# k and q of two head pairs handled together, six first-layer blocks held in SBUF, and a second phase that begins with results in SBUF, in a planned attention and feed-forward kernel

## The chip, the cores and the metric

The kernel runs on one core of a Trainium2 chip. The metric is device time in microseconds (us) of one execution. The engines are TensorE (PE in the profile; its weight loads are PEld), VectorE (DVE), ScalarE (ACT), GpSimd (POOL) and SyncE (SP), on whose queue all DMAs are issued. SBUF is the memory on the chip, PSUM holds what matmuls accumulate, and DRAM is outside.

## The reference

A linear attention over 8 batches, 8 heads, 576 positions and 64 columns per head, and then a feed-forward layer on its 4608 tokens of 512 columns, all in float32:

```python
q_s = softmax(q, axis=-1)            # over the 64 columns
k_s = softmax(k, axis=2)             # over the 576 positions of a batch
kv = einsum('bhsd,bhse->bhde', k_s, v)
x = einsum('bhsd,bhde->bhse', q_s, kv)     # then heads side by side: (4608, 512)
h = x @ w_in                               # 512 x 2048
g = where(h >= 1, h, where(h <= -1, 0, (h + 1) ** 2 / 4))
out = g @ w_out                            # 2048 x 512
```

## The kernel before

**Tiles.** The 4608 tokens are nine chunks of T = 512. A chunk's x is four pieces, one for each pair of heads (128 columns). The first layer makes h transposed, in 16 blocks f of 128 of the 2048 columns; the second layer adds each block into four PSUM banks o0 to o3 of 128 tokens by 512 columns. To keep float32 accuracy every operand is split into a rounded high part and the low rest, and a product is three matmuls (high x low, high x high, low x high). So one block's second layer is 4 banks x 3 matmuls of 128x512 (L1439), and its first layer in a plain chunk 4 pieces x 3 (L1240). In a row of the trace gh and gl are the parts of g, wh and wl those of w_out, qh and ql those of q.

**Stages.** Chunks 0, 1 and 2 are done plainly. In chunk 0 `weights` loads w_in and w_out from the inputs, splits them and stores the w_in blocks (512 KB each) to DRAM copies; chunks 1 and 2 fetch these again. While they do, `split` makes sums of weight blocks, ss, and their parts w_s (casts on ScalarE, L591; low parts on GpSimd, L596), which go to DRAM too. Chunks 3 to 8 are three pairs: `two_first_layers` makes the first layers of both chunks of a pair with seven instead of eight products (Strassen's scheme; tiles hA, hb, hC), out of sums of x. For these the chunks' x (xo, stored to xk by L963) is loaded again into xc by `x_sums` (L1143), combined (L1158), cast to its high part on ScalarE (L1170) and given its low part (L1175). The x parts lie in fourteen places x0 to x13 of SBUF, which chunks 0 to 2 also use: chunk 2's four pieces lie in x10 to x13, so that the first pair's x10 to x13 can be written only when chunk 2's last first layer has read them. Of a pair only the first chunk's g goes straight into the second layer. The second chunk's is spilled to DRAM (`keep`, L1400), loaded again (`recall`, L1411) and multiplied in a second phase, 16 blocks of 12 matmuls, behind the pair's products. It uses the same four banks, which `evict` copies into osb tiles first (two buffers; L379 on ScalarE, L381 on VectorE) and stores (L1497): the third copy needs the first one's store to have landed.

**Attention of a piece** (`attention`, from chunk 2 on). k's maximum over a batch's rows is taken in two steps: k_max over five column groups in three operations of VectorE (L724, L726, L727), and then over the partitions, for chunks 2 to 4 through two transposes on TensorE with a reduction between (L765, L769, L773), for chunks 5 and on by a `partition_all_reduce` on GpSimd (L776). Then k_sub (L780, VectorE), k's exponential (L785, ScalarE), the kv matmuls (L795, ten for each head pair; two pairs share one PSUM tile), 1/sum (L810, L812) and the two parts of kv (L829, L840). q's maximum and sum go over 32 partitions' groups: a reduction (L873, L891), four copies of 32 partitions and one combination (q_both, L861 and L862), the application on GpSimd (L882), exponential (L887), reciprocal (L899, L904), a transpose (L908), its two parts (L923, L927), the x matmuls (L939), and x's parts (L952 on ScalarE, L956 on VectorE).

**The order.** All instructions are written out by a planner (`Plan`). Each operation has an engine, a duration in us, a due time and what it depends on; buffers are `Ring`s. `order` makes a list schedule, and `settle` shifts the order for 450 turns (`late`, `early`), moving some operations near one point of time at random each turn, within the first 120 us of the plan. Transfers are planned with 2.6 us ahead of the first byte and 310 KB per us. Engines work in this order; a late instruction holds those queued behind it.

## Time and profile before

| what | value |
|---|---|
| runs shown | 868.74, 870.13 and 870.80 us, median 870.13 |
| the profiled execution, its own time | 870.23 us |
| its span in the trace | 868.5 us |
| TensorE busy | 842.0 us, 97% of the span |
| VectorE, ScalarE, GpSimd busy | 554.7, 478.4 and 298.3 us |
| mean granted TensorE clock | 0.991 |
| DMA | 172.70 MB |

In the views a row of waits gives the engine, its line, whom it waited for, the total, the number of times and the longest. A row of the timeline gives start and duration, engine, line, operation, output and inputs by the program's names (without the number of the buffer), and in brackets the idle time before it with what ended it. A row of a stretch gives the busy time (and count) of PE, PEld, DVE, ACT and POOL, then the granted clock, the DMA engines' busy share and GB/s.

### The profile page before, as it was taken

How to read it: one execution, taken by the hardware profiler on the slowest of the kernel's cores; microseconds unless marked ns; L12 is line 12 of the kernel's file. 1: busy time of each engine (PE TensorE's matmuls, PEld its weight loads, DVE VectorE, ACT ScalarE, POOL GpSimd, SP SyncE). 2: the span in 40 equal slices, each digit the busy share in tenths (PEclk: the TensorE clock that was granted, in tenths of full speed). 3: DMA queues.
4: the chain of work that ended last, by engine and by line, in shares of the span. 5: the costliest groups of instructions: out<-in, count | busy, mean ns of one | idle time of the engine just before them, and what ended most of it. 6: DMA issues, size and time to landing. Idle time of an engine off the chain costs nothing.

```text
span 868.5 us, 12535 instructions
## 1 busy us (share of the span) xinstructions
PE 842.0 (97%) x4272; PEld 685.4 (79%) x4272; DVE 554.7 (64%) x1199; ACT 478.4 (55%) x842; POOL 298.3 (34%) x265
## 2 busy tenths in 40 slices
PE   8999998999999997999999899999999999999998
PEld 6678777888887776788878788888887888888886
DVE  7788788888787745887699454777763024554300
ACT  7888745555545536565568344556574344545522
POOL 5656544344537314211212321112256730000153
PEclk9999999999999998999999999999999999999999
DMA  8999936646576527666757634557456335454332
GB/s 329 293 310 331 318 137 231 219 170 200 203 255 217 184 98 247 238 204 237 237 172 227 234 121 165 182 171 240 171 185 228 122 122 169 161 168 146 112 118 86
DMA packets 68176, 172.70 MB, mean 199 GB/s; under 512 B 7568, under 2 KB 7824, under 8 KB 68112
## 3 DMA queue, kind: packets, MB, share of 16 engines
q1 hardware_dynamic: 68112, 171.90, 58.0%
q8 instruction: 34, 0.56, 0.3%
q14 instruction: 30, 0.25, 0.1%
HBM read 126.78 MB, written 45.09 MB: 198 GB/s over the span
## 4 chain that ended last, share of the span: by engine, by line
PE 80%; DVE 8%; DMA 7%; ACT 2%; POOL 2%; issue 2%; POOLq 0%; SPq 0%; DVEq 0%; ACTq 0%
PE o L1439 38%; PE hA L1292 14%; PE h L1240 10%; PE hC L1292 7%; PE hb L1292 3%; PE x L939 3%; DMA st<-in_w 2%; PE kv L795 2%; DMA out<-osb 1%; DMA k<-in_k 1%; DMA xk<-xo 1%; PE warm L1612 1%; DVE qrzo L861 1%; DVE gl L1428 1%; DVE m L726 1%
## 5 line engine op out<-in xcount | busy, mean ns | idle before, releaser
L1439 PE MATMUL o<-wl,gh 128*128 128x512 f32 x576 | 229.0, 398 | 8.6 <-ACT gh L1423 4.7
L1439 PE MATMUL o<-wh,gl 128*128 128x512 f32 x576 | 226.6, 393 | 1.4 <-DVE gl L1428 1.2
L1439 PE MATMUL o<-wh,gh 128*128 128x512 f32 x576 | 225.5, 391 | 0.0
L1240 PE MATMUL h<-x,w 128*128 128x512 f32 x576 | 147.5, 399 | 4.1 <-DVE x L956 2.4
L1292 PE MATMUL hA<-x,w 128*128 128x512 f32 x576 | 147.3, 392 | 1.2 <-DVE c L1316 1.2
L1439 PEld LDWEIGHTS o<-wl,gh 128*128 128x128 f32 x576 | 109.0, 189 | 33.2 <-ACT gh L1423 5.4
L1439 PEld LDWEIGHTS o<-wh,gl 128*128 128x128 f32 x576 | 108.8, 189 | 27.8 <-DVE gl L1428 3.9
L1240 PEld LDWEIGHTS h<-x,w 128*128 128x128 f32 x576 | 107.0, 190 | 28.4 <-DVE x L956 3.0
L1292 PEld LDWEIGHTS hA<-x,w 128*128 128x128 f32 x576 | 107.3, 188 | 24.8 <-DVE c L1316 2.0
L1439 PEld LDWEIGHTS o<-wh,gh 128*128 128x128 f32 x576 | 109.0, 189 | 21.6
L1428 POOL TENSOR_TENSOR gl<-gs,gh 128x512 fp32r<-128x512 f32 x39 | 50.3, 1291 | 165.7 <-PE o L1439 122.6
L1384 ACT ACTIVATE r<-r 128x512 f32<-128x512 f32 x144 | 90.9, 632 | 3.9
L882 POOL TENSOR_TENSOR q<-q,qrz 128x512 f32<-128x512 f32 x36 | 39.6, 1101 | 107.3 <-DVE qrz L904 65.6
L1292 PE MATMUL hC<-x,w 128*128 128x512 f32 x288 | 73.8, 391 | 0.4 <-DVE gl L1428 0.3
L882 POOL TENSOR_TENSOR q<-q,qm 128x512 f32<-128x512 f32 x36 | 39.5, 1100 | 91.2 <-DVE qm L862 39.0
L1423 ACT CAST gh<-gs 128x512 fp32r<-128x512 f32 x48 | 29.9, 622 | 72.9 <-PE o L1439 57.5
L1381 ACT ACTIVATE r<-c,half 128x512 f32<-128x512 f32 x48 | 34.7, 722 | 60.8 <-DVE c L1316 60.7
L1292 PEld LDWEIGHTS hC<-x,w 128*128 128x128 f32 x288 | 53.7, 188 | 13.1 <-DVE gl L1428 1.7
L1381 ACT ACTIVATE r<-h,half 128x512 f32<-128x512 f32 x48 | 33.0, 687 | 48.9 <-PE h L1240 48.7
L1316 DVE TENSOR_TENSOR c<-hC,sn_P 128x512 f32<-128x512 f32 x24 | 16.6, 690 | 56.3 <-PE hC L1292 56.3
L1175 POOL TENSOR_TENSOR x<-xc,x 128x512 fp32r<-128x512 f32 x27 | 35.5, 1327 | 33.6 <-ACT x L1170 26.1
L1387 DVE SCALAR_TENSOR_TENSOR h<-h,r 128x512 f32<-128x512 f32 x48 | 33.1, 691 | 20.1 <-ACT r L1384 19.9
(126 smaller groups left out, 1241.2 us busy)
## 6 DMA issues: line engine op xcount, KB each, us to landing
w<-b SPq DMA_DIRECT2D x56, 512.0 KB, 4.6
w<-s SPq DMA_DIRECT2D x48, 512.0 KB, 3.6
st<-in_w SPq DMA_DIRECT2D x32, 512.0 KB, 6.1
g<-c SPq DMA_DIRECT2D x48, 256.0 KB, 2.6
gs<-g SPq DMA_DIRECT2D x48, 256.0 KB, 2.6
v<-in_v SPq DMA_DIRECT2D x32, 325.0 KB, 5.4
q<-in_q SPq DMA_DIRECT2D x36, 256.0 KB, 3.4
out<-osb SPq DMA_DIRECT2D x35, 256.0 KB, 3.3
```

The source lines that it names most:

```text
L795: nc.tensor.matmul(t["kv"][d, :], t["k"][r, j, d], t["v"][r, j, i * (D + 1) : (i + 1) * (D + 1)], start=(j == 0), stop=(j == KJ - 1), tile ...
L882: nc.gpsimd.tensor_tensor(t["qf"], t["qf"], at, alu)
L939: nc.tensor.matmul(t["x"][:, :, p0:p1], lhs, rhs[:, :, p0:p1], start=(i == 0), stop=(i == 2),)
L1175: eng.tensor_tensor(x[:, 1, :], t["xc"][:, at, :], f32(x[:, 0, :]), ALU.subtract)
L1240: nc.tensor.matmul(t["h"], lhs, rhs, start=(at == 0 and i == 0), stop=(at == NPAIR - 1 and i == 2),)
L1292: nc.tensor.matmul(banks[b]["h"], lhs, rhs, start=(begins and not kk and not m), stop=(ends and kk == 1 and m == 2), skip_group_check=True,)
L1381: nc.scalar.activation(t["r"], t["h"], AF.Relu, bias=half[:, :1], scale=0.5)
L1384: nc.scalar.activation(t["r"], t["r"], AF.Square)
L1387: nc.vector.scalar_tensor_tensor(t["h"], t["h"], 1.0, t["r"], ALU.max, ALU.min)
L1423: nc.scalar.copy(t["gh"], t["h"])
L1428: eng.tensor_tensor(t["gl"], t["h"], f32(t["gh"]), ALU.subtract)
L1439: nc.tensor.matmul(outs[c, j], lhs[:, s], rhs, start=(f == 0 and i == 0), stop=(f == NF - 1 and i == 2),)
```

## The change

1. **Two head pairs as one piece.** From chunk 2 on `attention_two` takes the place of `attention`. k_max is one tensor_reduce for each head pair. The second reduction (k_top), the sum and reciprocal of kv, q_both's copies (now on 32 columns) and q's reciprocal are done once for two pairs. A piece's two all-reduces stand one behind the other on GpSimd. Loads and due times are arranged anew (k 45 us ahead of q in the pairs; chunk 2's pieces are entered within chunk 1).
2. **HELD.** Blocks 1, 3, 5, 7, 9 and 11 of w_in are written in chunk 0 to the x places x10, x11, x12, x13, x8 and x9 and used in chunk 1 from there; their six loads of 512 KB go.
3. **The second phase** begins with blocks 14 and 15, whose g stays in SBUF: two stores and two loads of 256 KB less in each of the three pairs. Then follow blocks 0 to 13.
4. **The planner** adds a margin of 1.2 us to the end of stores to DRAM copies and of loads from them; a few durations are set anew; `settle` picks its point near a planned idle time of TensorE, by its length, anywhere in the plan.

The issued DMAs go from 473 to 455; the matmuls are the same.

```diff
+HELD = {1: 10, 3: 11, 5: 12, 7: 13, 9: 8, 11: 9}
...
-    TURNS, SEARCHED = 450, 120.0
+    TURNS = 450
 
     PATIENCE = 0.2
 
-    RELUCTANT = 3.0
+    RELUCTANT, MARGIN = 3.0, 1.2
...
+        op.margin = self.MARGIN
+        return op
...
+                op.end = self.gap([used["wire"]], us, op.start + self.FIRST) + us + op.margin
...
-                about = rng.uniform(0.0, self.SEARCHED)
+                pe = sorted((o.start, o.end) for o in order if o.engine == "PE")
+                idle = [(b[0], b[0] - a[1]) for a, b in zip(pe, pe[1:]) if b[0] > a[1] + 0.05]
+                about = rng.choices([x for x, _ in idle], [x for _, x in idle])[0]
+                about -= rng.uniform(0.0, 8.0)
...
+                if f in HELD:
+                    flat = x_room(HELD[f]).rearrange("p i t -> p (i t)")
+                    wr[0, f] = wr[1, f] = flat.rearrange("p (q i t) -> p q i t", q=2, i=2)
+                else:
+                    ws_tile((0, f))
...
+        late = START + STEP * (NF - 2 + f) if f in HELD else due
+        made["stored", f] = plan.save(0.45, late, store, [g], 512)
...
+            if c == 1 and f in HELD:
+                made[c, f] = made[f, 0]
+            else:
+                made[c, f] = fetch((c, f), due - 1.5 * STEP, blocks[f], [made["stored", f]])
...
+    def attention_two(c, h, kdue, qdue):
+
+        two = 2 * h, 2 * h + 1
+        n = f"{c}_{h}"
+        t = {pr: {} for pr in two}
+        b = {}
...
+        def k_max(i):
+            def emit():
+                if not i:
+                    b["m"] = wk.tile([P, 2, P], F32, tag="m2", name=f"m2_{n}")
+                k = t[two[i]]["k"].rearrange("p j d -> p d j")
+                nc.vector.tensor_reduce(b["m"][:, i, :], k, AX.X, ALU.max)
+
+            return emit
...
+        def k_top():
+            b["mx"] = sm.tile([P, 2], F32, tag="mx", name=f"mx_{n}", bufs=1)
+            nc.vector.tensor_reduce(b["mx"], b["mt"][:, 0:2, :], AX.X, ALU.max)
...
+        def k_all(i):
+            def emit():
+                t[two[i]]["mb"] = m = b["m"][:, i, :]
+                nc.gpsimd.partition_all_reduce(m, m, P, bass_isa.ReduceOp.max)
+
+            return emit
...
+        def kv_z():
+            z = sm.tile([P, 2], F32, tag="z2", name=f"z_{n}", bufs=2)
+            nc.vector.tensor_scalar(z, b["kv"][:, :, D], EPS, None, ALU.add)
+            b["rz"] = sm.tile([P, 2], F32, tag="rz2", name=f"rz_{n}", bufs=2)
+            nc.vector.reciprocal(b["rz"], z)
...
+            for i, pr in enumerate(two):
+                tag = ("k", "st1")[h]
+                loads[pr, "k"], rooms[pr, "k"] = load(
+                    pr, "k", k[c - KT, pr], [P, KJ, P], 320, kdue + 6 * i, tag
+                )
+                loads[pr, "v"], rooms[pr, "v"] = load(
+                    pr, "v", v[c, pr], [P, KJ, P + 2], 325, kdue + 33 + 3 * i, "v"
+                )
+            for i, pr in enumerate(two):
+                km = do("DVE", 0.8, kdue + 6 * i, k_max(i), loads[pr, "k"], *maxed, port=True)
+                maxed = [km]
+                if not i:
+                    rm.take(km)
+                loads[pr, "m"] = km
...
+                alls = [
+                    do("POOL", 13.6, kdue + 1 + 14 * i, k_all(i), loads[pr, "m"], made[NF - 1, 1])
+                    for i, pr in enumerate(two)
+                ]
+                subs = [
+                    do("DVE", 0.9, kdue + 16 + 14 * i, k_sub(pr), alls[i], port=True)
+                    for i, pr in enumerate(two)
+                ]
+                rm.free(*subs)
...
+            exps = [do("ACT", 0.74, kdue + 20 + 12 * i, k_exp(pr), subs[i]) for i, pr in enumerate(two)]
+            ra = ring("ps a", 1)
+            at = kdue + 34
+            deps = [loads[pr, "v"] for pr in two]
+            mm = do("PE", 1.68, at, kv_mms, *exps, *deps, *ra.wait())
+            ra.take(mm)
...
+        def q_both(what, alu, tag):
+            def emit():
+                part = b[what]
+                other = sm.tile([P, 2, nrow], F32, tag="qo2", name=f"{what}o_{n}", bufs=1)
+                b[what] = sm.tile([P, 2, nrow], F32, tag=tag, name=f"{what}b_{n}", bufs=1)
+                for g in range(NQ):
+                    r, o = (slice(x * QB, (x + 1) * QB) for x in (g, g ^ 1))
+                    nc.vector.tensor_copy(other[r], part[o])
+                nc.vector.tensor_tensor(b[what], part, other, alu)
+
+            return emit
...
+        both = do("DVE", 1.0, qdue + 2, q_both("qm", ALU.max, "qb2"), one, other, *rqb.wait(), port=True)
+        rqb.take(both)
+        rqa.free(both)
+        subs = [
+            do("POOL", 1.08, qdue + 4, q_rows(i, "qm", ALU.subtract), both, port=True)
+            for i in range(2)
+        ]
+        rqb.free(*subs)
...
+        users = [prev, made["stored", f] if c < 2 else None, made.get(("whole", c, f))]
+        users = [o for o in users if o]
+        if c > 1 or f not in HELD:
+            rws.free(*users)
+        elif c:
+            ring(f"x{HELD[f]}", 1).free(*users)
...
+            for h in range(2):
+                base, kbase = 20 + 4.8 * h, 13 + 5.2 * h
+                attention_two(c, h, START + STEP * kbase, START + STEP * base)
+            return
...
+            attention_two(c + i % 2, i // 2, at - 45, at)
...
+            if (c, p) == (1, NF // 4 - 1):
+                prepare(2)
...
+            kept = []
+            for i, unit in enumerate((three, four)):
+                d = middle(c + 1, f + i, due + 11 + 4 * i, *unit, kept=True)
+                if p == NF // 2 - 1:
+                    kept.append((f + i, unit[0], d))
+                else:
+                    keep(c + 1, f + i, due + 13 + 4 * i, unit[0], d)
...
-        for f in range(NF):
-            due = begin + step * 8 + step * 3 / NF * f
-            t, d = recall(c + 1, f, due)
-            ring("gs", NGS).free(second_layer(c + 1, f, due + 4, t, d, kept=True))
+        for i, f in enumerate([x[0] for x in kept] + list(range(NF - 2))):
+            due = begin + step * 8 + step * 3 / NF * i
+            t, d = kept[i][1:] if i < 2 else recall(c + 1, f, due)
+            last = second_layer(c + 1, f, due + 4, t, d, True, not i, i == NF - 1)
+            ring("gs", NGS).free(last)
```

Three places of the new order. First VectorE at the end of chunk 0, between the last q part of chunk 1's attention (ql_1_3) and x7's low half, the last piece of chunk 1's x. Before, nineteen rows lead from the one to the other; these are the last twelve (the first digit in a name is the chunk, the second the head pair, or the block for h and r):

```order
L727 TENSOR_TENSOR m2_2_2_1617<-m2_2_2_1617,k_2_2_1367 128x128
L873 TENSOR_REDUCE qm_2_2_1623<-q_2_2_1580 128x16
L1387 SCALAR_TENSOR_TENSOR h_0_15_1547<-h_0_15_1547,r_0_15_1597 128x512
L780 TENSOR_TENSOR k_2_1_1490<-k_2_1_1490,mt_2_1_1592 128x640
L861 COPY qmo_2_2_1643<-qm_2_2_1623 32x16 x4
L862 TENSOR_TENSOR qm_2_2_1644<-qm_2_2_1623,qmo_2_2_1643 128x16
L891 TENSOR_REDUCE qz_2_1_1660<-q_2_1_1551 128x16
L861 COPY qrzo_2_1_1686<-qz_2_1_1660 32x16 x4
L862 TENSOR_TENSOR qrz_2_1_1687<-qz_2_1_1660,qrzo_2_1_1686 128x16
L899 TENSOR_SCALAR qrz_2_1_1687<-qrz_2_1_1687 128x16
L904 RECIPROCAL qrz_2_1_1687<-qrz_2_1_1687 128x16
L956 TENSOR_TENSOR x7_1650<-x_1_3_1626,x7_1650 128x512
```

Now all of it is:

```order
L945 TENSOR_TENSOR ql_1_3_1596<-tp_1_3_1561,qh_1_3_1579 128x512
L1252 TENSOR_REDUCE m2_2_1_1598<-k_2_2_1463 128x128
L1416 TENSOR_REDUCE qa_2_0_1414<-q_2_1_1570 128x16
L1427 COPY qmo_2_0_1613<-qa_2_0_1414 32x32 x4
L1428 TENSOR_TENSOR qmb_2_0_1614<-qa_2_0_1414,qmo_2_0_1613 128x32
L1288 TENSOR_TENSOR k_2_0_1482<-k_2_0_1482,mt_2_0_1573 128x640
L1288 TENSOR_TENSOR k_2_1_1518<-k_2_1_1518,mt_2_0_1573 128x640
L974 TENSOR_TENSOR x7_1625<-x_1_3_1606,x7_1625 128x512
```

What moved: the reduction, copies and reciprocal for chunk 2's sum of q (qz, qrz) stand behind x7's low half now, q's maximum and its copies come once instead of twice, k_max is one row instead of three, and both k_sub of a piece stand ahead of x7.

Second, ScalarE ahead of the first pair, from x10's cast to gh of block 13 of chunk 2. Before:

```order
L1170 CAST x10_3674<-xc_3_0_2609 128x512
L1170 CAST x12_3683<-xc_3_0_2609 128x512
L591 CAST w_s_7_1_3686<-ss_7_3576 128x2x256
L785 ACTIVATE k_5_0_2826<-k_5_0_2826 128x640
L379 COPY xo_4_3_3740<-x_4_3_3715 128x512
L1381 ACTIVATE r_2_13_3748<-h_2_13_3692,half_93 128x512
L1384 ACTIVATE r_2_13_3748<-r_2_13_3748 128x512
L1170 CAST x1_3758<-xc_3_1_3713 128x512
L1423 CAST gh_2_13_3766<-h_2_13_3692 128x512
```

Now:

```order
L1188 CAST x10_3477<-xc_3_0_2538 128x512
L1188 CAST x12_3482<-xc_3_0_2538 128x512
L392 COPY xo_4_3_3499<-x_4_3_3484 128x512
L1757 ACTIVATE r_2_13_3509<-h_2_13_3441,half_93 128x512
L1294 ACTIVATE k_5_1_2716<-k_5_1_2716 128x640
L614 CAST w_s_7_0_3527<-ss_7_3454 128x2x256
L1760 ACTIVATE r_2_13_3509<-r_2_13_3509 128x512
L614 CAST w_s_7_1_3555<-ss_7_3454 128x2x256
L1801 CAST gh_2_13_3557<-h_2_13_3441 128x512
L1188 CAST x1_3582<-xc_3_1_3516 128x512
```

Both w_s of the seventh sum stand here now, and x1 of the next x sums has gone behind gh. The exponential is that of chunk 5's second head pair, not of its first.

TensorE at the same place, from block 14's first layer on. Before:

```order
L1240 MATMUL h_2_14_3761<-x10_1805,w_2_14_3499 128x512 x3
L1240 MATMUL h_2_14_3761<-x12_2199,w_2_14_3499 128x512 x3
L1240 MATMUL h_2_14_3761<-x11_1890,w_2_14_3499 128x512 x3
L1240 MATMUL h_2_14_3761<-x13_2264,w_2_14_3499 128x512 x3
L1439 MATMUL o_2_0_2924<-wl13_1028,gh_2_13_3766 128x512
```

Now:

```order
L1611 MATMUL h_2_14_3518<-x10_1872,w_2_14_3304 128x512 x3
L1611 MATMUL h_2_14_3518<-x12_2180,w_2_14_3304 128x512 x3
L1304 MATMUL kv_5_0_3532<-v_5_0_3344,k_5_0_2697 64x65 x10
L1304 MATMUL kv_5_0_3532<-v_5_1_3347,k_5_1_2716 64x65 x10
L1611 MATMUL h_2_14_3518<-x11_1932,w_2_14_3304 128x512 x3
L1611 MATMUL h_2_14_3518<-x13_2239,w_2_14_3304 128x512 x3
L1817 MATMUL o_2_1_2786<-wl12_1006,gh_2_12_3445 128x512
```

The kv matmuls of chunk 5's first piece (two head pairs) stand between the halves of the first layer; behind it come eight more matmuls on block 12 and only then those on gh_2_13, which before follow at once.

Third, SP ahead of the first pair's output stores (osb_3_0 and osb_3_1). Before:

```order
L690 DMA q_7_0_5232<-in_q 128x512
L690 DMA k_7_2_5269<-in_k 128x640
L690 DMA v_7_0_5273<-in_v 128x650
L690 DMA v_7_1_5280<-in_v 128x650
L1400 DMA g15_159<-c22_3_7_5171 128x512
L1497 DMA out<-osb_3_0_5287 128x512
L1497 DMA out<-osb_3_1_5301 128x512
L690 DMA k_7_3_5314<-in_k 128x640
```

Now:

```order
L1240 DMA k_7_2_4944<-in_k 128x640
L1240 DMA v_7_0_4949<-in_v 128x650
L1240 DMA v_7_1_4954<-in_v 128x650
L1240 DMA k_7_3_4958<-in_k 128x640
L1875 DMA out<-osb_3_0_4972 128x512
L1875 DMA out<-osb_3_1_4985 128x512
L1787 DMA gs_4_1_5001<-g1_145 128x512
```

The load of q and the spilled g of block 15 are gone from ahead of the stores; k's second load stands ahead of them instead of behind.

347 lines of the change are left out of this document (274 added, 73 removed).

## The prediction

> **What bounds the kernel now.** I read the page of the profile first, then TensorE's waits, then stretches of 25 us, and last the engines' timelines where TensorE stands. The profiled execution took 870.23 us, its span is 868.5 us, so 1.7 us lie around the span; the median of the runs shown is 870.13 us, 0.1 from it. I make the sum against the 870.2 us of the profiled execution. The page's first two lines:
>
> ```profile
> span 868.5 us, 12535 instructions
> PE 842.0 (97%) x4272; PEld 685.4 (79%) x4272; DVE 554.7 (64%) x1199; ACT 478.4 (55%) x842; POOL 298.3 (34%) x265
> ```
>
> TensorE is busy for 97% of the span, and the change takes no matmul away. What can be won is therefore the remaining time, and slow time inside the busy time. The longest waits of TensorE (total, times, longest):
>
> ```profile
> PE o L1439 <- ACT gh L1423: 4.7, 1, 4.7
> PE o L1439 <- ACT osb L379: 3.9, 2, 3.1
> PE h L1240 <- DVE x L956: 2.4, 1, 2.4
> ```
>
> These are three places. In the same three stretches the granted clock (the column behind the five engines) is below 1:
>
> ```profile
> 125.00:150.00 25.00, 22.00 (x128) 18.14 (x127) 21.88 (x55) 14.54 (x28) 10.73 (x11) 0.93 0.63 222
> 325.00:350.00 25.00, 19.68 (x107) 15.44 (x108) 15.77 (x36) 15.59 (x29) 11.74 (x10) 0.86 0.74 252
> 475.00:500.00 25.00, 21.91 (x95) 18.19 (x94) 13.77 (x32) 9.93 (x20) 8.33 (x7) 0.93 0.70 232
> ```
>
> The clock is part of the price of a wait, as TensorE's timeline at the third place (start, duration) shows:
>
> ```profile
> 478.06 0.39 PE L1439 MATMUL o<-wh,gh 128*128 128x512 f32 x1
> 478.29 0.39 PE L1439 MATMUL o<-wh,gl 128*128 128x512 f32 x1
> 481.77 0.80 PE L1439 MATMUL o<-wl,gh 128*128 128x512 f32 x1 [3.09 <-ACT osb L379]
> 482.36 0.63 PE L1439 MATMUL o<-wh,gh 128*128 128x512 f32 x1
> 482.79 0.63 PE L1439 MATMUL o<-wh,gl 128*128 128x512 f32 x1
> ```
>
> Ahead of the wait a 128x512 matmul starts every 0.23 us (478.06, 478.29), behind it every 0.43 (482.36, 482.79). A clock of 0.93 over 25 us is about 25 x 0.07 x 2 = 3.5 us at half clock, and costs half of that, 1.7 us; 0.86 (325 to 350) is twice as long and costs 3.4 us. I call the places A (chunk 0 to 1), B (before the first pair) and C (its second phase).
>
> **A: VectorE is late with x7.** TensorE, then VectorE:
>
> ```profile
> 128.88 1.53 PE L795 MATMUL kv<-v,k 128*64 128x65 f32 x40 [0.63 <-issue]
> 132.78 5.30 PE L1240 MATMUL h<-x,w 128*128 128x512 f32 x15 [2.37 <-DVE x L956]
> ```
> ```profile
> 121.75 0.68 DVE L927 TENSOR_TENSOR ql<-tp,qh 128x512 fp32r<-128x512 f32 x1
> 122.35 0.66 DVE L873 TENSOR_REDUCE qm<-q 128x16 f32<-128x512 f32 x1
> 123.05 0.71 DVE L861 COPY qmo<-qm 32x16 f32<-32x16 f32 x4
> 127.98 0.80 DVE L780 TENSOR_TENSOR k<-k,mt 128x640 f32<-128x640 f32 x1
> 132.09 0.63 DVE L956 TENSOR_TENSOR x<-x,x 128x512 fp32r<-128x512 f32 x1
> ```
>
> TensorE loses 0.63 + 2.37 us and 1.7 of clock, 4.7 in all. It waits for the low half of x7 (L956), which VectorE has written at 132.72, 10.3 us after it finished the last ql of chunk 1 (121.75 + 0.68 = 122.4). Between them it is never idle: what lies there is k_max, q_max, q_sum, copies and subtractions for chunk 2. The groups that the change replaces:
>
> ```profile
> L724 DVE TENSOR_TENSOR m<-k 128x256 f32<-128x256 f32 x24 | 17.8, 742 | 3.8 <-DMA k<-in_k 3.6
> L726 DVE TENSOR_TENSOR m<-m 128x128 f32<-128x128 f32 x24 | 12.3, 512 | 0.8
> L727 DVE TENSOR_TENSOR m<-m,k 128x128 f32<-128x128 f32 x24 | 9.2, 384 | 0.8
> L733 DVE TENSOR_REDUCE nm<-k 128x1 f32<-128x576 f32 x4 | 3.0, 749 | 1.4 <-DMA k<-in_kt 1.4
> ```
>
> One k_max is 0.742 + 0.512 + 0.384 = 1.64 us now. In its place comes one tensor_reduce over 128x640, which no row of before shows in that layout (its last axis lies 128 elements apart). The nearest row is the 128x576 one at 0.749 us, by length 0.749 x 640/576 = 0.83 us; the upper bound is what it replaces, 1.64, a lower one the 0.66 us of q_max's 128x512. I take 0.83, by the nearest row. In the changed order six rows remain between that ql and x7's low half: k_max 0.83, q_max 0.66, four copies 0.71, their combining operation at 0.2 (32 columns, where one copy of 16 takes 0.71/4 = 0.18), two k_sub of 0.80: 4.0 us, and x7's low half is there at 4.0 + 0.63 = 4.6. TensorE has the x product behind ql (three passes over 512 columns, 0.7) and 15 matmuls of 0.23 before it needs x7: 4.2 us. That leaves 0.4 us, with hand-overs 0.5 (0 to 1.5), and no slow clock. A falls from 4.7 to 0.5: **-4.2**.
>
> [...]
>
> The rest of what VectorE saves (24 k_max, half of the 32-partition copies, reciprocals) is some 60 us of its time by the same rows, but at B and C, the two longer waits, ScalarE and a store come last. I cost that at nothing; TensorE's own queue hides it, and if that cover were gone it would show as further waits on gl or x, which is the 1.5 us added below.
>
> **B: a cast behind a queue on ScalarE.** TensorE, then ScalarE:
>
> ```profile
> 321.96 2.88 PE L1240 MATMUL h<-x,w 128*128 128x512 f32 x12
> 329.53 0.79 PE L1439 MATMUL o<-wl,gh 128*128 128x512 f32 x1 [4.69 <-ACT gh L1423]
> ```
> ```profile
> 322.83 1.30 ACT L1170 CAST x<-xc 128x512 fp32r<-128x512 f32 x2 [10.58 <-PE h L1240]
> 324.56 0.73 ACT L785 ACTIVATE k<-k 128x640 f32<-128x640 f32 x1
> 325.20 0.56 ACT L379 COPY xo<-x 128x512 f32<-128x512 f32 x1
> 325.67 0.69 ACT L1381 ACTIVATE r<-h,half 128x512 f32<-128x512 f32 x1
> 328.89 0.58 ACT L1423 CAST gh<-h 128x512 fp32r<-128x512 f32 x1 [0.25 <-DVE h L1387]
> ```
>
> x10 and x12 may be overwritten only when chunk 2's last h has read them (ScalarE's 10.58 us of idling ends there). Behind these two casts stand a w_s, k's exponential, xo, two relu steps and x1, and only then gh of f = 13, for which TensorE stands 4.69 us; with 3.4 of clock B costs 8.1. In the changed order the queue is much the same (x10, x12, xo, relu, k's exponential, w_s, square, w_s, gh, and x1 now behind it), but TensorE has more in front of the o matmuls that need gh: the kv products of a whole piece stand between the halves of h, and nine o matmuls of f = 12 behind them. Counted from the end of h's matmuls on x10: ScalarE reaches the end of k's exponential at 0.65 + 0.65 + 0.56 + 0.69 + 0.73 = 3.3 us; TensorE has until then three matmuls and ten of kv (1.53/40 x 10 = 0.38), 1.1 us, and stands about **2.2 us**, a wait that is not there before. Behind it lie 0.38 + 15 x 0.23 = 3.8 us of work, so TensorE runs dry at 7.1. ScalarE's second w_s waits for GpSimd, and with it gh, whose readers are the o matmuls. GpSimd, then the subtraction on VectorE that waits for the second all-reduce:
>
> ```profile
> 304.77 0.72 POOL L776 PARTITION_ALL_REDUCE m<-m  x1 [6.81 <-DVE z L810]
> 312.79 1.09 POOL L559 TENSOR_TENSOR ss<-sw 128x256 f32<-128x256 f32 x1 [7.30 <-issue]
> 323.54 1.29 POOL L1175 TENSOR_TENSOR x<-xc,x 128x512 fp32r<-128x512 f32 x1 [8.95 <-ACT x L1170]
> 331.48 0.95 POOL L776 PARTITION_ALL_REDUCE m<-m  x1 [6.66 <-issue]
> ```
> ```profile
> 335.85 0.81 DVE L780 TENSOR_TENSOR k<-k,m 128x640 f32<-128x640 f32 x1
> ```
>
> GpSimd makes two low halves (1.29 each) from 0.7 on, then three ss operations of at most 1.09: 6.6; then w_s 0.65 and gh 0.58, 7.8: I take 0.5 us of waiting (0 to 0.7). The first summed pair's w now goes out behind a load that waits for xk4_3's store (the SP queue is in order): 0 to 1.8 us more, I take 0.7. B comes to 2.2 + 0.5 + 0.7 = 3.4 without slow clock: **-4.7**, and between -1.7 (all three at their upper ends and 1.7 of clock) and -8.1.
>
> **C: the output buffers.** ScalarE, and the four stores' way to landing (min/median/max):
>
> ```profile
> 473.93 1.28 ACT L379 COPY osb<-o 128x512 f32<-128x512 f32 x2
> 481.13 1.26 ACT L379 COPY osb<-o 128x512 f32<-128x512 f32 x2 [4.04 <-DMA out<-osb]
> ```
> ```profile
> DMA to landing us min/median/max: 4.0/5.0/6.5
> ```
>
> The third copy of the banks waits for the first one's store, which took the 6.5 us of the maximum, and TensorE waits 3.09 us for the bank; with 1.7 of clock 4.8. In the changed order TensorE has the same twelve matmuls as cover (those of f = 14 and 15 on o0 and o1), so only the store's time counts. Immediately ahead of it stand k, v, v, k (1290 KB) where q, k, v, v and a spilled g (1482 KB) stood; and the second phase's first two results need no store and load, 12 DMAs of 256 KB less in all. I take the median, 5.0: the gap is 3.09 - 1.5 = 1.6 (0.6 by the minimum, 3.1 if nothing changes): -1.5, and -1.7 of clock. The fourth bank's matmuls now follow at once and its store is issued after the third's, for which I give back 0.3: **-2.9** (bounds 0 and -4.8).
>
> Everywhere else: the six blocks kept in SBUF save six 512 KB loads in chunk 1, where none of the three waits lies; the planner's margin of 1.2 us on transfers moves their issue, not their length. I cost both at nothing, hidden by TensorE's queue, and add 1.5 us, half a wait like C's, for new waits in an order that is new everywhere.
>
> **The clock rule.** At A an idle of 2.37 us was followed by half clock, at C one of 3.09. [...] The remaining 2.2 at B and 1.6 at C lie between 0.63 (A's first) and 2.37. I add 0.8, about one chance in four for each of two falls of 1.7.
>
> **Sum.** 870.2 - 4.2 - 4.7 - 2.9 + 1.5 + 0.8 = **860.7 us**.
>
> **The rivals.**
> 1. Only A goes (chance 0.17). For: A is arithmetic on VectorE, B and C hang on ScalarE's queue and a store's landing, which spread from 4.0 to 6.5. Time 870.2 - 4.2 = 866.0.
> 2. All three go nearly whole, without slow clock and without new waits (0.12): A whole, B down to 1.6, C to 0.5. For: the cover at A is 0.4 us short of whole, and C's store at the minimum of 4.0 leaves 0.6. Against: B's kv wait is in the order. 870.2 - 4.7 - 6.5 - 4.3 = 854.7.
> 3. Slower (0.07): GpSimd's two all-reduces of a piece, now queued back to back. One holds GpSimd from 6.81 us before its row to 7.30 behind it, 297.96 to 312.79, 14.8 us. If two take 29.6 from the same 298.0 on, the second is done and GpSimd free at 327.6. h's last matmul on x10 (322.8 now) ends 4.2 earlier, near 318.6. k's exponential then ends at 327.6 + 0.80 + 0.73 = 329.1, while TensorE arrives at kv at 319.7: 9.4 us. GpSimd's low halves and ss (5.9) end at 333.5, gh at 334.7, TensorE dry at 329.1 + 3.8 = 332.9: 1.8 more, with 3.4 of clock 14.6 against B's 8.1: 870.2 - 4.2 + 6.5 = 872.5, C left as it is. Behind VectorE's subtractions stand gl of f = 11 and the min of f = 13, which would be held as well. It decides where the second all-reduce ends later than x10's last reader. Against it: the changed order has one pair of switching instructions around the two, and the subtraction at 335.85 follows its all-reduce (331.48) by 4.4 us, so I expect 14.8 + 4.4 = 19.2, an end near 317.
> 4. No change (0.07): new waits in the other stages take what A to C give; 870. Against: the waits of A to C are single long ones that their rows explain, and none of them needs a gain of the planner to go.
>
> The forecast keeps 0.57. Faster by over 0.2% (1.7 us, about what a measurement of this kernel can tell): 0.57 + 0.17 + 0.12 = 0.86; same 0.07; slower 0.07. The range takes in rivals 1 and 2 and the bounds of B and C: 854 to 867. The forecast's own range is 857 to 864.5.
>
> **What would show it.** Right at A: no TensorE wait on x's low half above 1 us, and k_max near 0.83. Right at B: TensorE stands about 2.2 us at the kv products of chunk 5, and not at gh of f = 13. Right at C: the wait for osb is below 2 us. Rival 3 shows as GpSimd idle twice around two all-reduces and TensorE waiting behind w_s. I am wrong if VectorE still ends a wait above 2 us, if slow clock remains in more than one stretch, or if new waits exceed 3 us.

## The result, and the profile after

| what | before | changed kernel |
|---|---|---|
| median of 20 runs each (lowest to highest) | 869.37 us (867.22 to 873.07) | 865.24 us (862.26 to 869.52) |
| ratio after to before, 95% interval | | 0.9949 (0.9935 to 0.9962) |
| the profiled execution, its own time | 870.23 us | 865.27 us |
| its span | 868.5 us | 863.5 us |
| mean granted clock | 0.991 | 0.994 |

The kernel became faster by 0.5%, 4.1 us of the medians and 5.0 us of the two profiled executions. The forecast was 9.5 us. The sign holds, and 865.24 us lies in the range (854 to 867), but just outside the forecast's own, narrower one (857 to 864.5); the size is about half. One run of e5 below took 1393.57 us at a granted clock of 0.556, and e5's time goes by the other three.

The engines' line of the changed kernel's page:

```profile
PE 843.1 (98%) x4272; PEld 684.5 (79%) x4272; DVE 507.0 (59%) x949; ACT 476.3 (55%) x838; POOL 306.3 (35%) x273
```

Already here something is unexpected: the matmuls are the same 4272, yet TensorE is busy 1.1 us longer than the 842.0 us of before, although less of the span has a low clock. VectorE has lost 250 instructions and 47.7 us (some 60 forecast).

The two longest waits of TensorE, and the one for osb (total, times, longest):

```profile
PE h L1611 <- DVE gl L1806: 4.4, 2, 4.1
PE hA L1668 <- DVE c L1692: 2.2, 1, 2.2
PE o L1817 <- ACT osb L392: 0.6, 1, 0.6
```

Of the three waits of before little is left: none for x7's low half at A (2.4 us before), 0.6 for osb (3.9), and none for gh of f = 13 (4.7). Two others stand at the top. The stretches of 25 us (busy time and count of PE, PEld, DVE, ACT and POOL, granted clock, DMA share, GB/s):

```profile
25.00:50.00 25.00, 20.52 (x96) 16.05 (x96) 19.48 (x35) 18.06 (x34) 12.50 (x11) 0.86 0.78 259
125.00:150.00 25.00, 25.00 (x150) 20.43 (x149) 17.68 (x40) 14.75 (x28) 12.71 (x14) 1.00 0.62 213
325.00:350.00 25.00, 24.33 (x104) 19.01 (x103) 19.14 (x30) 16.72 (x31) 12.45 (x11) 1.00 0.94 328
425.00:450.00 25.00, 22.82 (x95) 18.26 (x95) 18.61 (x33) 13.10 (x22) 2.56 (x3) 0.93 0.63 220
475.00:500.00 25.00, 24.75 (x111) 20.04 (x112) 12.34 (x24) 12.32 (x23) 9.24 (x8) 1.00 0.52 179
```

The stretches of A, B and C are whole again: the clock is 1.00 in each, and TensorE idles 0, 0.7 and 0.25 us. What B keeps, 1.6 us of waiting at the kv products, now lies in the stretch ahead (300 to 325, clock 1.00). Two stretches, 25 to 50 and 425 to 450, now have a clock below 1, where the kernel before has 1.00 in both. In the kernel before the first of them read:

```profile
25.00:50.00 25.00, 22.97 (x119) 17.53 (x118) 19.99 (x41) 20.59 (x38) 13.37 (x11) 1.00 0.92 304
```

To add gains and losses in one currency I take the starts of all matmuls in the trace: the time from one start to the next, less the time that a matmul of that shape takes in the undisturbed course (0.227 us for 512 columns). The sum of the excess is 52.8 us before and 47.9 after; the difference, 4.9, is the gain in span (5.0) but for 0.1. By stretch, in us (e9 and e12 are two of the experiments below):

| stretch, us | before | after | e9 | e12 |
|---|---|---|---|---|
| 0 to 50 | 12.9 | 17.4 | 18.0 | 15.4 |
| 50 to 125 | 5.3 | 4.3 | 3.5 | 4.6 |
| 125 to 140 (A) | 5.3 | 1.0 | 0.8 | 0.8 |
| 140 to 300 | 7.2 | 4.7 | 3.9 | 3.9 |
| 300 to 340 (B) | 7.9 | 3.9 | 4.3 | 4.1 |
| 340 to 420 | 4.5 | 3.2 | 2.5 | 2.7 |
| 420 to 475 (D) | 1.8 | 7.0 | 5.8 | 3.6 |
| 475 to 490 (C) | 4.9 | 0.9 | 0.9 | 0.1 |
| 490 to the end | 3.0 | 5.6 | 2.5 | 2.0 |
| sum | 52.8 | 47.9 | 42.2 | 37.2 |

By these rows A, B and C gave 4.3, 4.0 and 4.0 us. The border at 475 us cuts through C, though: the changed kernel's wait of 0.63 us for osb ends at 474.87 and is counted in the row of D, so C gave 3.4, and the three together 11.7, where 11.8 had been forecast. The smaller waits around them gave 4.8 more. The losses are 4.5 in the first 50 us, 5.2 in the row of a place that I call D (4.6 without the wait for osb), and 2.6 in the long second phases at the end, which have no wait to show for it. What follows is about these three losses.

**The start.** TensorE and VectorE of the changed kernel:

```profile
33.76 2.93 PE L1611 MATMUL h<-x,w 128*128 128x512 f32 x6 [4.11 <-DVE gl L1806]
```
```profile
29.33 1.13 DVE L467 TENSOR_SCALAR st<-st 128x512 uint32<-128x512 uint32 x1 [0.41 <-DMA st<-in_w]
30.98 0.68 DVE L1763 SCALAR_TENSOR_TENSOR h<-h,r 128x512 f32<-128x512 f32 x1
33.02 0.68 DVE L1806 TENSOR_TENSOR gl<-h,gh 128x512 fp32r<-128x512 f32 x1
```

and VectorE of the kernel before, the min of the relu (h) and gl of the first block:

```profile
27.83 0.70 DVE L1387 SCALAR_TENSOR_TENSOR h<-h,r 128x512 f32<-128x512 f32 x1 [0.27 <-ACT r L1384]
29.18 0.69 DVE L1428 TENSOR_TENSOR gl<-h,gh 128x512 fp32r<-128x512 f32 x1
```

The min stood at 27.83 us, and stands at 30.98 now, behind the splitting of a weight block (L467 to L470) that itself waited 0.41 us for its load. gl comes 3.8 us later, TensorE waits 4.11 us, and a stretch at half clock follows (granted 0.50 from 34 to 38 us, 0.86 over the row above).

**D.** VectorE and TensorE near 428 us, in the first pair:

```profile
428.24 1.23 DVE L1252 TENSOR_REDUCE m<-k 128x128 f32<-128x640 f32 x1 [2.30 <-DMA k<-in_k]
429.38 0.68 DVE L1692 TENSOR_TENSOR c<-hA,sn_P 128x512 f32<-128x512 f32 x1
```
```profile
430.12 1.99 PE L1668 MATMUL hA<-x,w 128*128 128x512 f32 x6 [2.18 <-DVE c L1692]
431.91 0.63 PE L1817 MATMUL o<-wl,gh 128*128 128x512 f32 x1
432.34 0.63 PE L1817 MATMUL o<-wh,gh 128*128 128x512 f32 x1
```

VectorE works in its written order here: it stands 2.30 us before a k_max of chunk 6, whose k hasn't landed, and the addition c (L1692) stands behind it and begins at 429.38. TensorE needs c: 2.18 us of waiting, and then matmuls that start 0.43 us apart (431.91, 432.34) instead of 0.23, at a granted clock of 0.50 from 432 to 434 us. On SP's queue the k load goes out at 423.75 only, behind a load of w that waits from 416.8 to 422.9.

**The rate.** In the last second phase, with no wait anywhere, rows 24 matmuls apart, first of the kernel before and then of the changed one:

```profile
848.81 0.39 PE L1439 MATMUL o<-wl,gh 128*128 128x512 f32 x1
854.25 0.39 PE L1439 MATMUL o<-wl,gh 128*128 128x512 f32 x1
```
```profile
835.20 0.39 PE L1817 MATMUL o<-wl,gh 128*128 128x512 f32 x1
840.63 0.39 PE L1817 MATMUL o<-wl,gh 128*128 128x512 f32 x1
...
849.00 0.39 PE L1817 MATMUL o<-wl,gh 128*128 128x512 f32 x1
854.62 0.39 PE L1817 MATMUL o<-wl,gh 128*128 128x512 f32 x1
```

Before, 24 matmuls take 5.44 us (0.227 us each), here as elsewhere in the phase. After, 5.43 at the first and 5.62 at the second (0.234). The border lies where the phase passes from w_out's block 7 to block 8: blocks 0 to 7 run at the old rate, 8 to 15 at 0.2333 us by the median of their starts. There are 8 blocks x 9 chunks x 12 = 864 such matmuls, and 864 x 0.0062 = 5.4 us by estimate. This hides in busy time, so no view of waits shows it. The two groups of blocks lie in two places of SBUF, each block's high and low part in a tile of 2048 bytes of a partition, one tile behind the other. In the programs as allocated, wl8, the low part of block 8, starts at byte 196352 before and at 196768 after: small tiles ahead of it (k_top's, kv's and q_both's) changed size. The tiles of blocks 0 to 7 start at 9984 in both. 9984 and 196352 are multiples of 256, and so are the starts of all tiles of their groups; 196768 is 160 past one.

### The profile page after: what moved, and what is told of

The parts are those of the page before. It is cut to its first block, busy times and chain, and to the rows that moved or that the text cites. A ratio compares the mean times of both kernels' runs of the same rounds, so it can differ in the third digit from the quotient of the medians.

```text
span 863.5 us, 12245 instructions
## 1 busy us (share of the span) xinstructions
PE 843.1 (98%) x4272; PEld 684.5 (79%) x4272; DVE 507.0 (59%) x949; ACT 476.3 (55%) x838; POOL 306.3 (35%) x273
## 4 chain that ended last, share of the span: by engine, by line
PE 83%; DMA 6%; DVE 3%; ACT 3%; POOL 2%; issue 2%; SPq 0%; POOLq 0%; DVEq 0%; ACTq 0%
PE o L1817 41%; PE hA L1668 14%; PE h L1611 12%; PE hC L1668 7%; DMA st<-in_w 4%; PE hb L1668 3%; PE x L1491 2%; PE kv L1304 2%; DMA out<-osb 1%; ACT gh L1801 1%; DMA q<-in_q 1%; DMA k<-in_k 1%; POOL wl L497 0%; POOL x L497 0%; ACT r L1757 0%
## 5 line engine op out<-in xcount | busy, mean ns | idle before, releaser
L1611 PE MATMUL h<-x,w 128*128 128x512 f32 x432 | 111.3, 399 | 4.6 <-DVE gl L1806 4.4
L1611 PEld LDWEIGHTS h<-x,w 128*128 128x128 f32 x432 | 80.2, 190 | 22.9 <-DVE gl L1806 5.2
L1801 ACT CAST gh<-gs 128x512 fp32r<-128x512 f32 x42 | 26.1, 622 | 69.1 <-PE o L1817 61.0
L1806 POOL TENSOR_TENSOR gl<-gs,gh 128x512 fp32r<-128x512 f32 x37 | 47.7, 1290 | 42.1 <-ACT gh L1801 34.3
L1436 POOL TENSOR_TENSOR q<-q,qmb 128x512 f32<-128x512 f32 x28 | 29.6, 1072 | 90.8 <-DVE qmb L1428 66.5
L1193 POOL TENSOR_TENSOR x<-xc,x 128x512 fp32r<-128x512 f32 x30 | 38.9, 1306 | 56.7 <-ACT x L1188 55.6
L1436 POOL TENSOR_TENSOR q<-q,qzb 128x512 f32<-128x512 f32 x28 | 30.3, 1097 | 79.3 <-DVE qzb L1458 39.0
L1806 POOL TENSOR_TENSOR gl<-c,gh 128x512 fp32r<-128x512 f32 x4 | 5.2, 1289 | 122.2 <-PE o L1817 118.4
```

Source lines behind the costliest of these rows:

```text
L1193: eng.tensor_tensor(x[:, 1, :], t["xc"][:, at, :], f32(x[:, 0, :]), ALU.subtract)
L1436: nc.gpsimd.tensor_tensor(qf, qf, at, alu)
L1611: nc.tensor.matmul(t["h"], lhs, rhs, start=(at == 0 and i == 0), stop=(at == NPAIR - 1 and i == 2),)
L1801: nc.scalar.copy(t["gh"], t["h"])
L1806: eng.tensor_tensor(t["gl"], t["h"], f32(t["gh"]), ALU.subtract)
```

## The experiments

My theory after the result: A to C did what was forecast, and three things that the prediction had at nothing took it back: the new order's waits at the start and at D (with their half clock), and a slower matmul rate that comes from the address of w_out's second group of tiles. The rivals: the rate is contention from other engines; the three-operation k_max would have done as well; the start's loss comes from the planner's new search or from HELD. Every kernel below computes the whole result. e1 to e4 ran on one chip beside 17 runs of the kernel before (median 871.33), e5 to e8 beside 9 (870.56), e9 to e11 beside 12 (869.34), e12 beside 11 (869.61).

**e1, the changed kernel again**, as a control.

> The changed kernel once more, as the control of the three beside it. Theory: the gain at A, B and C is real and part of it is given back by two new waits, one at about 29 to 34 us (TensorE for a bank that VectorE's gl frees, 4.1 us and 1.7 us of half clock behind it) and one at 428 to 430 us (for VectorE's addition c, 2.2 us and 1.7 us of half clock). Then both stand again in this profile at the same places, and the time is 865 (863.5 to 866.5). Rival: they are chance of one execution; then one of them is missing or under 1 us here.

865.51 us, ratio 0.9943 (0.9923 to 0.9962). The same waits at the same places: 4.1 us for gl at the start, 2.3 for c at D. They belong to the order and not to one execution. One thing differs: behind B's wait, 1.19 us for xo in both, e1's matmuls start 0.43 us apart (at 323.58 and 324.01) and the clock from 300 to 325 is 0.93, where the execution above has 0.23 us and 1.00.

**e2, the addition ahead of k_max at D.** Behind `settle`, an operation x of the finished order (by its number) is taken ahead of another, y; here the addition c ahead of k_max:

```diff
     order = plan.settle()
+    def ahead(x, y):
+        ...
+        order.insert(order.index(y), x)
+    ahead(1730, 2107)
```

> The changed kernel with one instruction moved: VectorE makes the addition c of the second product set (block 11 of chunk 4) ahead of the k_max of chunk 6 that waits for its load of k, instead of behind it. Theory: TensorE's wait of 2.2 us at 428 and the half clock behind it go, 3.9 us: 861.3 (860 to 862.5). Rival: what k_max starts (the all-reduce on GpSimd, k's exponential) is then late and the wait comes back further on, or VectorE is the bound of this stretch anyway: 864 to 865.5.

863.16 us, 0.9914 (0.9891 to 0.9938), 2.4 us under e1, with intervals that overlap; it lies between the time of the theory and that of the rival. VectorE of e2 at D, and another stretch of it:

```profile
428.01 0.69 DVE L1692 TENSOR_TENSOR c<-hA,sn_P 128x512 f32<-128x512 f32 x1 [0.73 <-PE hA L1668]
429.63 1.32 DVE L1252 TENSOR_REDUCE m<-k 128x128 f32<-128x640 f32 x1 [0.93 <-DMA k<-in_k]
```
```profile
75.00:100.00 25.00, 25.00 (x123) 20.21 (x123) 18.16 (x35) 19.02 (x36) 12.13 (x11) 0.93 0.83 273
```

The addition runs at 428.01, k_max behind it still waits for its load and holds nobody. TensorE's wait there and the half clock behind it are gone, so c behind k_max is their cause, shown. In the table's measure the stretch from 420 to 475 falls from 7.8 in e1 to 3.7; 1.2 of these 4.1 us is a shorter wait for osb, which falls into it (1.57 us in e1, 0.39 here). The half clock between 75 and 100 us (0.93 above), which e1 doesn't have, costs 1.6 us and follows a wait of 1.67 us at 73.8 (1.11 in e1). It lies 350 us ahead of the moved instruction, so it is no price of the edit (e8 and e12 have the same edit and no half clock there).

**e3, k_max in three operations**, each pair's own, the rest as changed:

```diff
-                nc.vector.tensor_reduce(b["m"][:, i, :], k, AX.X, ALU.max)
+                nc.vector.tensor_tensor(two_, k[:, 0:2, :], k[:, 2:4, :], ALU.max)
+                nc.vector.tensor_tensor(m, two_[:, 0, :], two_[:, 1, :], ALU.max)
+                nc.vector.tensor_tensor(m, m, k[:, 4, :], ALU.max)
```

> The changed kernel in the same order, with k_max as three tensor_tensor operations again in place of the one tensor_reduce. Theory: k_max's length is on no path that sets the end, since one takes 1.30 us in the profile where I had put 0.83 and A has no wait for all that; three operations at 1.64 us cost 0.3 at most where TensorE waits for VectorE behind a k_max (at 428): 865.2 to 865.8, that is 0 to 0.6 above the control. Rival: the tensor_reduce is what freed VectorE, and the waits at A come back: 1.5 to 4 us above the control, with a wait of TensorE on x7 at 125 to 130 us.

867.11 us, 0.9957 (0.9943 to 0.9971), 1.6 us over e1. The groups in e3 (instructions, busy time, mean ns of one, idle time before), and k_max's one group in the changed kernel:

```profile
L1254 DVE TENSOR_TENSOR m<-m 128x128 f32<-128x128 f32 x24 | 14.1, 590 | 0.8
L1253 DVE TENSOR_TENSOR m<-k 128x256 f32<-128x256 f32 x24 | 13.7, 572 | 2.5 <-DMA k<-in_k 2.4
L1255 DVE TENSOR_TENSOR m<-m,k 128x128 f32<-128x128 f32 x24 | 11.6, 485 | 0.8
```
```profile
L1252 DVE TENSOR_REDUCE m<-k 128x128 f32<-128x640 f32 x24 | 31.2, 1303 | 2.5 <-DMA k<-in_k 2.3
```

The tensor_reduce takes 1.303 us and the three together 0.590 + 0.572 + 0.485 = 1.65, so the new form is 0.34 us shorter, not the 0.81 of the forecast. At A there is no wait for x7 in e3 either; but the three take only 1.1 us there, the tensor_reduce of the changed kernel 1.3, so that place doesn't tell the two forms apart. The waits that e3 has more of than e1 are small and elsewhere (gh 1.5 us in all where e1 has none, ql 1.2 against 0.3). My theory had no more than 0.6 us for this and is missed by its number; the rival's time is met, but not its wait. The intervals of e1 and e3 overlap, so the 1.6 us itself isn't sure.

**e4, the search at the start again.** `settle` picks its point as before:

```diff
-                about = rng.choices([x for x, _ in idle], [x for _, x in idle])[0]
-                about -= rng.uniform(0.0, 8.0)
+                about = rng.uniform(0.0, 120.0)
```

> The changed kernel with the planner's search put back to the first 120 us (the rest of part 4 as changed); the order is a new one everywhere. Theory: the new choice of the point took the search away from the start, which now costs 17.3 us of TensorE's time in the first 50 us where it cost 12.9; with the old choice the wait on gl at 30 us is under 2 us and the first 50 us cost 13 to 14, 3 to 4 us less than in the control; elsewhere some waits return, so that the time is 862 to 867. Rival: the start is late for another reason (loads, the stores of the held blocks), and the first 50 us cost 16 to 18 us again.

865.96 us, 0.9941 (0.9917 to 0.9965), no different from e1. The longest waits of e4's TensorE and its second stretch:

```profile
PE o L1814 <- ACT osb L389: 3.1, 1, 3.1
PE et L768 <- ACT k L389: 2.5, 1, 2.5
PE hA L1665 <- DMA w<-b: 2.3, 1, 2.3
```
```profile
25.00:50.00 25.00, 21.01 (x108) 16.35 (x107) 18.15 (x34) 18.56 (x35) 12.23 (x11) 1.00 0.82 279
```

The wait of 4.1 us at the start is gone, the clock there is 1.00, and the first 50 us cost 14.4 in the table's measure, 3.0 less than in the changed kernel and a little over the 13 to 14 of the theory. In its place stand waits that are short or missing in the changed kernel: 2.5 us for k at 31 us, 3.1 for osb, which half clock follows (0.92 from 450 to 475 us), and 2.3 for a load of weights. So the old search does better at the start and worse elsewhere; the sum is the same.

**e5 to e7 and e9, e10, the address of w_out's second group of tiles.** In the changed kernel one small tile ahead of the group is made larger, nothing else:

```diff
-            b["mx"] = sm.tile([P, 2], F32, tag="mx", name=f"mx_{n}", bufs=1)
+            b["mx"] = sm.tile([P, 16], F32, tag="mx", name=f"mx_{n}", bufs=1)[:, 0:2]
```

This is e5: wl8 starts at byte 196800, a multiple of 64. e9 has 32 columns (196864, a multiple of 256), e10 has 64 (196992, a multiple of 128 but not of 256). e7 is e5 with the edit of e2. e6 is the other way round, in the kernel before:

```diff
-            other = sm.tile([P, nrow], F32, tag="qo", name=f"{tag}o_{n}", bufs=1)
+            other = sm.tile([P, nrow + 8], F32, tag="qo", name=f"{tag}o_{n}", bufs=1)[:, :nrow]
```

32 bytes more, and wl8 starts at 196384 instead of 196352.

> The changed kernel with one small tile (mx) taking 64 bytes of each partition instead of 32, so that all that lies behind it, the w_out blocks 8 to 15 among it, starts at a multiple of 64 bytes again as in the kernel before; order and work are unchanged. In the profile of the changed kernel a second-layer matmul on blocks 8 to 15 starts every 0.2338 us and one on blocks 0 to 7 every 0.2272, in the kernel before 0.2273 on both. Theory: the start address of the operand sets this, 864 matmuls x 0.0066 = 5.7 us come back: 859.8 (858.5 to 861) where the control took 865.5, and the gap between starts is 0.227 on blocks 8 to 15. Rival: it is where these blocks lie among the other buffers, or what runs beside them; then nothing changes (864.5 to 866.5).

> The kernel before with one small tile (the copies of q_both) 32 bytes longer, so that the w_out blocks 8 to 15 start 32 bytes past a multiple of 64 as in the changed kernel; order and work are those of before. Theory: it becomes slower by 864 x 0.0066 = 5.7 us, 0.65% (0.5 to 0.8%), with 0.234 us between matmuls on these blocks. Rival: no difference (within 0.2%).

> The changed kernel with both the 64 bytes for mx and the addition c moved ahead of k_max. Theory: the two are independent, 5.7 and 2.4 us: 857.4 (856 to 859). Rival: with the matmuls faster the waits grow by what they win (VectorE, ScalarE or loads set the pace), 859.5 to 862.

> The changed kernel with the small tile mx taking 128 bytes of each partition: the w_out blocks 8 to 15 then start at a multiple of 256 bytes (wl8 at 196864), as in the kernel before (196352) and as blocks 0 to 7 do. At 32 bytes past a multiple of 64 (196768, 196384) and at 64 past one of 128 (196800) the matmuls on them took 0.233 us from start to start. Theory: a multiple of 128 or 256 makes them fast again: 0.227 on blocks 8 to 15, 864 x 0.006 = 5.3 us less than the control, 860.3 (859 to 862). Rival: what counted in the kernel before is the place within 2048 bytes (1792 there for all operands of TensorE, 256 here); then 0.233 again and 865.5.

> The same with 256 bytes for mx: the blocks start 128 past a multiple of 256 (wl8 at 196992). If multiples of 128 are enough, 0.227 between the matmuls on blocks 8 to 15; if it takes 256, or the place within 2048 bytes, 0.233.

Again rows of TensorE 24 matmuls apart in blocks 8 to 13 of the last second phase; for e6 two pairs, one in blocks 0 to 7 and one behind. e5, e6, e9, e10:

```profile
848.81 0.39 PE L1817 MATMUL o<-wh,gh 128*128 128x512 f32 x1
854.41 0.39 PE L1817 MATMUL o<-wh,gh 128*128 128x512 f32 x1
```
```profile
835.00 0.39 PE L1439 MATMUL o<-wh,gh 128*128 128x512 f32 x1
840.44 0.39 PE L1439 MATMUL o<-wh,gh 128*128 128x512 f32 x1
...
850.01 0.40 PE L1439 MATMUL o<-wh,gh 128*128 128x512 f32 x1
855.61 0.40 PE L1439 MATMUL o<-wh,gh 128*128 128x512 f32 x1
```
```profile
845.68 0.39 PE L1817 MATMUL o<-wl,gh 128*128 128x512 f32 x1
851.12 0.39 PE L1817 MATMUL o<-wl,gh 128*128 128x512 f32 x1
```
```profile
848.92 0.40 PE L1817 MATMUL o<-wh,gl 128*128 128x512 f32 x1
854.52 0.40 PE L1817 MATMUL o<-wh,gl 128*128 128x512 f32 x1
```

| kernel | start of the tiles | 24 matmuls | time, us | ratio (95%) |
|---|---|---|---|---|
| before | multiple of 256 | 5.44 | | |
| changed, e1 | 160 past one | 5.62 | 865.51 | 0.9943 (0.9923 to 0.9962) |
| e5 | 192 past one | 5.60 | 865.77 | 0.9934 (0.9908 to 0.9959) |
| e6 (before, shifted) | 32 past one | 5.60 | 873.96 | 1.0043 (1.0018 to 1.0069) |
| e9 | multiple of 256 | 5.44 | 860.27 | 0.9897 (0.9855 to 0.9939) |
| e10, one run | 128 past one | 5.60 | 863.98 | |

e6 makes the kernel before slower by 0.43% (0.18 to 0.69; my theory had 0.65) with 32 bytes and nothing else, and the matmuls are slower only in the blocks whose tiles moved: the address is the cause, shown, and contention falls, since the engines' work is the same. My first form of the theory (a multiple of 64 is enough) fell with e5. e9 is back at 5.44 and e10 isn't, so a multiple of 128 isn't enough either; and the place within 2048 bytes isn't what counts, since it is 1792 in the kernel before and 256 in e9. What is left is a multiple of 256, by the five places tried (0, 32, 128, 160 and 192 past one). e7 (862.55 us, 0.9903, 0.9887 to 0.9919) is 3.2 us under e5 by the exchange of e2, which won 2.4 there; it still has the slow rate, and with it misses its theory's 857.4.

**e8, the start.** e7, and on VectorE and ScalarE six operations of the first blocks' relu, split and gh are taken ahead of others, so that the first min and gl aren't queued behind a split that waits:

```diff
+    for x, y in ((233, 251), (216, 251), (250, 241), (217, 241), (218, 242), (252, 242)):
+        ahead(x, y)
```

> The kernel of the run before with six instructions of the start moved as well: on VectorE the join of one weight block, the first block's min and its gl ahead of the shift that waits for its load, or of the second block's min, on ScalarE the next block's scale and the first gh ahead of the second square. Theory: TensorE's wait of 4.1 us for the bank at 29 to 34 us is the order's doing, gl comes about 1.8 us earlier, and the next weight block too: 1.5 to 2.5 us less than the run before, 855.4 (854.5 to 857). Rival: the loads of weights set the start (DMA engines busy 0.87 to 0.99 there), what is won at 30 us is waited for until 100 us: within 0.7 us of the run before.

861.34 us, 0.9887 (0.9861 to 0.9913). The min begins at 29.49 instead of 30.98, TensorE waits 2.73 us for gl instead of 4.11, and in the second stretch the clock is still 0.93. The start's cost falls by 1.5 us in the table's measure, and the time by 1.2, within the intervals of e7 and e8 and between the theory's 1.5 to 2.5 and the rival's 0.7. So the queue on VectorE is a part of the loss at the start, and not all of it.

**e11, without HELD.**

```diff
-HELD = {1: 10, 3: 11, 5: 12, 7: 13, 9: 8, 11: 9}
+HELD = {}
```

> The changed kernel without held blocks (six loads of 512 KB in chunk 1 come back; the order is a new one everywhere). Theory: the held blocks save loads that nobody waited for, so that no wait of TensorE on a load of w appears between 130 and 320 us, and the time is that of the changed kernel but for the luck of the order: 863 to 868. Rival: the saved loads are what made the small waits of chunks 1 and 2 go (2.5 us between 140 and 300 us): they come back, 867 to 870.

864.06 us, 0.9935 (0.9913 to 0.9956), the same as the changed kernel. TensorE has no wait for a load of w_in in chunk 1. The planner makes another order out of it, without the waits at the start's gl and at D, but with 3.3 us for gh and 2.9 for ql, and about 4 us more between 50 and 100 us. What HELD itself is worth can't be told apart from the new order; together they change the time by less than the intervals.

**e12, what the runs point to**: the changed kernel with e9's tile, e2's edit and e8's six moves.

> The changed kernel with all three: mx at 128 bytes (w_out blocks 8 to 15 at a multiple of 256), the addition c ahead of k_max, and the six instructions of the start. The run with the last two took 861.3 with 0.2333 us between the matmuls on those blocks. Theory: 864 x 0.006 = 5.3 us come off unchanged, 856 (854.5 to 857.5), ratio to the kernel before 0.983 to 0.986. Rival: part of it is waited for again, since loads and VectorE are then reached earlier: 858 to 860.

856.12 us, ratio 0.9852 (0.982 to 0.9884): faster than both kernels, and the 856 of the theory. Its span is 852.8 us, and its page has:

```profile
PE 834.7 (98%) x4272; PEld 682.3 (80%) x4272; DVE 506.2 (59%) x949; ACT 476.4 (56%) x838; POOL 306.9 (36%) x273
```

TensorE is busy 8.4 us less than in the changed kernel with the same matmuls, which is the rate, the half clock at D and a part of that at the start.

## Why the prediction was right in sign and half in size

- **A, forecast -4.2, measured -4.3.** No wait for x7 and no half clock are left. But the working had two errors that cancel. VectorE's last ql of chunk 1 and x7's low half, and TensorE's first matmuls on x7, in the changed kernel:

```profile
129.95 0.68 DVE L945 TENSOR_TENSOR ql<-tp,qh 128x512 fp32r<-128x512 f32 x1
134.81 0.69 DVE L974 TENSOR_TENSOR x<-x,x 128x512 fp32r<-128x512 f32 x1
136.85 0.86 PE L1611 MATMUL h<-x,w 128*128 128x512 f32 x3
```

  x7's low half is there 4.9 us after the end of that ql (130.63), not 4.6, because k_max takes 1.3 us and not 0.83. TensorE needs it 6.2 us after that end, not 4.2, because it reaches the x product only 1.8 us behind ql. That the longer k_max costs nothing is luck of the order; what carries A is that 4.9 us of VectorE's work stand between ql and x7 where 10.3 stood. The row by which I priced k_max had its elements side by side and one result; here the last axis lies 128 elements apart and 128 results come out. It took 1.303/0.83 = 1.6 times as long, and no run shows which of the two costs it. The 1.303 lies between my 0.83 and the 1.64 of the three operations that it replaces, and by the means of e3 (1.65) the edit still won 0.34 us each.
- **B, forecast -4.7, measured -4.0.** The new wait at the kv products came as forecast, in two parts:

```profile
319.44 0.80 PE L1304 MATMUL kv<-v,k 128*64 128x65 f32 x20 [1.19 <-ACT xo L392]
320.66 0.80 PE L1304 MATMUL kv<-v,k 128*64 128x65 f32 x20 [0.41 <-ACT k L1294]
```

  1.19 + 0.41 = 1.6 us against 2.2. Its larger part is for the copy xo, which holds the PSUM tile, and not for k's exponential as I had it. There is none at gh of f = 13, and no half clock in this execution; e1 had it behind the same wait.
- **C, forecast -2.9, measured -3.4** (4.0 by the table's row, less the wait in the row of D). The wait for osb is 0.6 us (1.6 forecast; e1 showed 1.6, e3 1.9, e10 1.0), and the half clock is gone.
- **Rival 3** didn't come. GpSimd of the changed kernel, the two all-reduces of the piece in question and those of a later one:

```profile
289.01 1.43 POOL L1280 PARTITION_ALL_REDUCE m<-m  x2 [5.47 <-DVE h L1763]
433.52 1.51 POOL L1280 PARTITION_ALL_REDUCE m<-m  x2 [8.73 <-issue]
```

  GpSimd waits 27.87 us for ScalarE behind the first two, so the later ones show the price: from the end of the work ahead (424.80) to the next work, which starts at 443.50 after 8.47 us of idling, two hold GpSimd 18.7 us. One held it 14.8 in the kernel before; the rival had 29.6 for two, the forecast 19.2. In the piece in question the subtraction that needs the second all-reduce starts at 309.15, ahead of x10's cast (317.60), so the rival's condition isn't met.
- **The step that failed** is "Everywhere else": six loads and the planner's margin "at nothing", and 1.5 us "for new waits in an order that is new everywhere". The measured sizes: 4.5 us at the start and 3.4 at D (5.2, less 1.2 of rate, by after less e9, and 0.6 of C's wait), against 7.1 won where small waits went (4.8 by the table, and 2.3 more that the rate covers, again by after less e9). That is a loss of 0.8 together, where 1.5 and the clock's 0.8 had been put. That it is small is luck: it is the difference of terms several times its size that the forecast had not named. What is left of the error is the matmul rate, 5.4 us, for which the forecast had no term at all: 860.7 + 5.4 = 866.1, against 865.27 in the profiled execution. With the tiles back at a multiple of 256 (e9) the ratio is 0.9897, which makes 861.2 us of the 870.2, close to the forecast. The order of instructions shows no addresses, and the profile of before has no slow matmul that could have warned.
- **The signs of being wrong** that the prediction named all came, outside A to C: VectorE ends waits of 4.11 and 2.18 us, slow clock remains in two stretches (0.86 and 0.93), and a new wait exceeds 3 us (4.11). The nearest time among the rivals is that of rival 1 (866.0), by number alone: it leaves B and C as they were, and both went.
- **The clock rule.** At D idle times of 2.04 to 2.32 us were followed by half clock in five of six kernels with that wait (the changed one, e1, e3, e5, e9). In e10 it was not:

```profile
430.67 1.66 PE L1668 MATMUL hA<-x,w 128*128 128x512 f32 x6 [2.12 <-DVE c L1692]
432.16 0.40 PE L1817 MATMUL o<-wl,gh 128*128 128x512 f32 x1
432.39 0.39 PE L1817 MATMUL o<-wh,gh 128*128 128x512 f32 x1
```

  2.12 us, and the starts behind it are 0.23 apart. Over all fourteen traces the fifteen idle times of TensorE of 2.7 to 4.7 us were all followed by half clock, eight of the eleven from 2.0 to 2.5 us, and four of some forty from 1.0 to 1.9 us (the first 3 us of each kernel left out). The 0.8 us that I had added for B and C wasn't needed in the profiled execution; the falls came at the start and at D, where I had put none.

Open: the whole cause of the start's loss (six moves win 1.5 of the 4.5 us; the search and HELD, each undone, change the whole order with it), and the prices of the second phase's new first blocks and of the planner's margin by themselves, which weren't tried. A to C are read from the rows of before and after; no run undoes the change at one of them alone.
